# One tile for response and inputs: three sums of 384 columns in the spectral stage

## The chip, the cores and the metric

The kernel runs on one core of a Trainium2 chip. The core has five engines that work side by side, each through its own queue and in order: TensorE (matmuls, PE in the profile; its weight loads are PEld), VectorE (DVE), ScalarE (ACT), GpSimd (POOL) and SyncE (SP), which here only issues transfers. Matmuls read operands from SBUF and write sums to PSUM; ScalarE and VectorE read the sums from there. The metric is device time in microseconds (us); three runs of the kernel before took 1110.23, 1110.36 and 1110.42 us, median 1110.36.

## What is computed

With L = 2048 positions, D = 576 channels, N = 128 states and F = 4608 hidden units:

```python
x = A_u
xn = _layernorm(x, axis=-1)
return x + _A_ref(xn, ...) + _B_ref(xn, B_w1, B_w2)

# _B_ref: out = silu(xn @ w1) @ w2
# _A_ref: a long convolution for each channel
K = jnp.einsum("dn,dnl,dn->dl", Cc, exp(dt * A * l), dB).real
Kf = rfft(K padded to 2 * L)
Uf = rfft(xn padded to 2 * L)
y = irfft(Uf * Kf)[:L] + xn * Dskip
```

Two parts are added: a feed-forward block, which is most of the arithmetic, and a convolution of each channel with its own response K, done through a Fourier transform in stages that are matmuls.

## The kernel before

All large matmuls have float32 operands split in two parts of fewer bits, a high part `h` and a low part `l` (`h` is a rounding copy on ScalarE, `l` the difference on VectorE). A product is then three matmuls: high with high, high with low, low with high.

**The feed-forward block** (`ffn`) goes over two halves of the positions, nine chunks of four 128-wide slices of F, and two blocks of 512 positions. `up` makes a sum `ph` of 14 matmuls, 512 columns wide (lines 331 to 333), ScalarE takes its SiLU (`gf`, line 339) and its high part (`gh`, line 340), VectorE the low part (`gl`, line 342). `down` makes sums `po` of twelve matmuls, 288 columns wide (line 357), and VectorE adds them to `acc` (line 361).

**The convolution** (`side`) is a generator that is woven into the steps of `ffn`: `kgen` makes the response K and its first transform stage into a tensor `d1k` in HBM, `spread` does the first stage of the inputs into `d1u`, `spectral` does the middle of the transform and writes `d2`, `tail` does the last stage and adds the result to the outputs. `marks` and `tail_at` (lines 865 and 866) say at which shares of `ffn`'s steps each part is called. A planner that estimates each instruction's time then sets the order of each engine's queue, so a matmul of `spectral` stands between matmuls of `ffn` wherever the planner put it; `behind` ties an instruction after another one, and `high_priority` moves it up.

**The spectral stage** (`spectral`, line 730) has 32 steps `k`. For each, SyncE loads 128 rows of `d1u` and 128 rows of `d1k` (`load_part`, line 816: tiles `ur` and `kr`, 576 columns each, two buffers). `split_of` (line 809) makes `uh`, `ul`, `kh` and `kl`. `front` (line 735) multiplies both with the step's 128x128 matrix (`mk`, loaded for two steps at once into `mm`). It goes over the halves of the 576 channels, 288 columns (`HD`) each: a sum `pk` of the response, which ScalarE copies out in four pieces of 64 partitions into `ka` and `kb` (lines 750 to 753, a real and an imaginary part in two arrangements), then a sum `pu` of the inputs, which VectorE multiplies with `ka` and `kb` into `y` and `y2` (lines 756 to 758). The sums of `mm3` (line 821) have three matmuls, all recorded at line 826. Then VectorE adds `y` and `y2`, `split_of` splits the result, and one more matrix gives two sums `pb`, which ScalarE copies to `yo` (line 778) and GpSimd's queue writes to `d2`. `front(k + 1)` is called ahead of the `pb` of step `k`.

All sums of this stage take a buffer of the pool `pss`, which has three, a 2 KB bank for each partition: `pk`, `pu`, `pk`, `pu` and two `pb` for each step. `ps1` (two buffers) holds `ph`, `ps2` (three) holds `po`.

The first operands are loaded and split ahead of the others (line 762 and 766), and `ops` holds them for step 0.

Of the kernel before, what the change touches and what calls it, by code (L numbers as in the profile page):

```python
# [11 lines left out]
F32 = mybir.dt.float32  # L12
F32R = mybir.dt.float32r
# [6 lines left out]
P = 128  # L20
L = 2048
D = 576
# [2 lines left out]
NJ = 16  # L25
NKT = 4
HD = D // 2
NFT = FF // P
MAGIC = 12582912.0
TWO_PI = float(np.nextafter(np.float32(2 * math.pi), np.float32(0)))  # L30
# [13 lines left out]
def kernel(  # L44
# [21 lines left out]
    nc = tc.nc  # L66
    FT = 4
    NCH = NFT // FT

# [4 lines left out]
    def quarters(v, engines):  # L74

        for q in range(4):
            yield slice(32 * q, 32 * q + 32), v[q // 2, q % 2], engines[q % len(engines)]

    dram = ctx.enter_context(tc.tile_pool(name="dram", bufs=1, space=DRAM))
    d1u = dram.tile([32 * P, D], F32, name="d1u")  # L80
    d1k = dram.tile([32 * P, D], F32, name="d1k")
# [28 lines left out]
    pss = ctx.enter_context(tc.tile_pool(name="pss", bufs=3, space=PSUM))  # L110
# [31 lines left out]
    def behind(ins):  # L142
        return tc.issue_after(ins) if ins is not None else nullcontext()

    def spread(up):
# [3 lines left out]
        for j in range(NJ):  # L149
            src = up.tile([P, D], F32, tag="xr", name="xr")  # L150
            nc.sync.dma_start(src, dxn[:, j])
            for m in range(2):
# [5 lines left out]
                for h in range(2):  # L158
                    hs = slice(h * HD, (h + 1) * HD)
                    pu = pss.tile([P, 512], F32, tag="pss", name="pu")  # L160
                    nc.tensor.matmul(pu[:, :HD], s1[:, 0, :], sp[:, hs], start=True, stop=False)  # L161
                    nc.tensor.matmul(pu[:, :HD], s1[:, 1, :], sp[:, hs], start=False, stop=True)  # L162
                    nc.scalar.copy(u1[:, hs], pu[:, :HD])
                nc.gpsimd.dma_start(
# [15 lines left out]
    def store(t, j, engines):  # L180

        for hs in (slice(0, HD), slice(HD, D)) if j == NJ - 1 else (slice(0, D),):
            for ps, v, eng in quarters(ov, engines):
                eng.dma_start(v[:, j:j + 2] if len(t.shape) > 2 else v[:, j, hs], t[ps] if len(t.shape) > 2 else t[ps, hs])

    def norm(p0, js, xs):
# [4 lines left out]
        for i in range(n):  # L191
            for h in range(2):
                nc.vector.bn_stats(out=st[:, i, h, :], in_=xs[i][:, h * HD:(h + 1) * HD])
            nc.vector.bn_aggr(out=mv[:, i, :], in_=st[:, i, :, :])
# [253 lines left out]
    kl = yp = pa = tail_at = None  # L448
# [281 lines left out]
    def spectral():  # L730
        def operands(k):
            rows = slice(k * P, (k + 1) * P)
            return load_part(d1u[rows, :], "u"), load_part(d1k[rows, :], "k")

        def front(k):
            if k % 2 == 0:
                mm = kl.tile([P, 2, 4, P], F32R, tag="mm", name="mm")
                nc.gpsimd.dma_start(mm, cm23[:, k:k + 2])
                mats.append(mm)
            mk = mats[-1][:, k % 2]  # L740
            us, ks = ops.pop(k) if k in ops else (split_of(t, n) for t, n in zip(operands(k), "uk"))
            ka = kl.tile([P, D], F32, tag="ka", name="ka")
            kb = kl.tile([P, D], F32, tag="kb", name="kb", bufs=1)
            y = kl.tile([P, D], F32, tag="y", name="y", bufs=1)
            y2 = kl.tile([P, D], F32, tag="y2", name="y2", bufs=1)
            for h in range(2):
                hs = slice(h * HD, (h + 1) * HD)
                pk = pss.tile([P, 512], F32, tag="pss", name="pk")
                mm3(pk[:, :HD], [(mk[:, 0], mk[:, 1], ks)], hs)
                nc.scalar.copy(ka[:64, hs], pk[:64, :HD])  # L750
                nc.scalar.copy(ka[64:, hs], pk[:64, :HD])
                nc.scalar.mul(kb[:64, hs], pk[64:, :HD], -1.0)
                nc.scalar.copy(kb[64:, hs], pk[64:, :HD])
                pu = pss.tile([P, 512], F32, tag="pss", name="pu2")
                mm3(pu[:, :HD], [(mk[:, 0], mk[:, 1], us)], hs)
                nc.vector.tensor_mul(y[:, hs], pu[:, :HD], ka[:, hs])
                nc.vector.tensor_mul(y2[:64, hs], pu[64:, :HD], kb[:64, hs])
                nc.vector.tensor_mul(y2[64:, hs], pu[:64, :HD], kb[64:, hs])
            nc.vector.tensor_add(y, y, y2)
            return mk, split_of(y, "y")  # L760

        mats = []
        first = operands(0)
        yield 1.1
        with behind(pins["gh"]):
            ops = {0: [split_of(t, n) for t, n in zip(first, "uk")]}
        yield 1.12
        nxt = front(0)
        for k in range(32):
            mk, ys = nxt  # L770
            if k < 31:
                nxt = front(k + 1)
            yo = kl.tile([P, D], F32, tag="yo", name="yo")
            for h in range(2):
                hs = slice(h * HD, (h + 1) * HD)
                pb = pss.tile([P, 512], F32, tag="pss", name="pb")
                mm3(pb[:, :HD], [(mk[:, 2], mk[:, 3], ys)], hs)
                nc.scalar.copy(yo[:, hs], pb[:, :HD])
            nc.gpsimd.dma_start(d2.rearrange("(p k) d -> k p d", k=32)[k], yo)
            yield 1 + (k + 1) / 32  # L780
# [26 lines left out]
    yss = {}  # L807

    def split_of(t, tag):
        h = kl.tile([P, D], F32R, tag=tag + "h", name=tag + "h")  # L810
        l = kl.tile([P, D], F32R, tag=tag + "l", name=tag + "l")
        nc.scalar.copy(h, t)
        nc.vector.tensor_sub(l, t, h)
        return h, l

    def load_part(rows, tag):
        t = kl.tile([P, D], F32, tag=tag + "r", name=tag + "r")
        nc.sync.dma_start(t, rows)
        return t

    def mm3(dst, terms, hs):

        n = 0
        for sh, sl, (mh, ml) in terms:
            for st, mv in ((sh, mh), (sh, ml), (sl, mh)):
                nc.tensor.matmul(dst, st, mv[:, hs], start=n == 0, stop=n == 3 * len(terms) - 1)  # L826
                n += 1
# [35 lines left out]
    def side():  # L863
# [66 lines left out]
        with tc.tile_pool(name="kl", bufs=2) as kl:  # L930
            for at in spectral():
                yield marks[1] + (at - 1) * (marks[2] - marks[1])
# [90 lines left out]
```

## Time and profile before

| what | value |
| --- | --- |
| runs, median (lowest to highest) | 1110.36 us (1110.23 to 1110.42) |
| span of the profiled execution, first to last instruction | 1108.2 us |
| granted TensorE clock over the span | 1.000 |
| matmuls of the whole kernel | 9167 |
| matmuls of lines 357 / 331 to 333 | 3456 / 2072 |
| matmuls of line 826, `pk` / `pu` / `pb` | 192 / 192 / 192 |

The profile page gives the span of one profiled execution; its own time outside the span is not listed, and the median of the runs lies 2.16 us above the span. In the profile's rows, `L826 PE MATMUL pk<-kh,mm 128*128 128x288 f32` reads: line 826, TensorE, a matmul that writes `pk` from `kh` and the matrix `mm`, 128 rows by 128 columns of weights, 288 moving columns. In a timeline the first number is the start from the beginning of the span and the second the duration, both in us; rows are merged (x4) where the same instruction follows itself, and what stands in brackets is the engine's idle time before the row and what ended it. In a list of groups the numbers after the bar are the busy time in us, the mean of one in ns, and the idle time before in us. In a list of waits they are the total in us, how often, and the longest. The list of transfers ends each row with the median time in us from issue to landing.

### The profile page before, as it was taken

The page shows a single profiled execution, that of the slowest core. Times are in us where ns is not written, and L with a number is a line of the kernel's source. Part 1 is how long each engine was busy: PE and PEld are TensorE (multiplying, and loading weights), DVE is VectorE, ACT ScalarE, POOL GpSimd, SP SyncE. Part 2 cuts the span into 40 slices and gives each one's busy share as a digit, 9 for nine tenths or more (in the row PEclk, how much of TensorE's full clock was granted, in tenths as well). Part 3 has the DMA queues.
Part 4 walks back from the last instruction along what each step waited for, and adds up shares of the span by engine and source line. Part 5 has one row for each costly group of instructions (what it writes and reads, how often), then busy time and mean ns, then how long its engine had stood idle before and what let it go on. Part 6 is the DMA issues. An engine that isn't in the chain of part 4 may idle for free.

```text
span 1108.2 us, 22917 instructions
## 1 busy us (share of the span) xinstructions
PE 1102.2 (99%) x9167; PEld 997.5 (90%) x9167; DVE 916.6 (83%) x1543; ACT 706.9 (64%) x1222; POOL 72.1 (7%) x129
## 2 busy tenths in 40 slices
PE   9999999999999999999999999999999999999998
PEld 7989998899998899899999989999999999999887
DVE  7799899999999999999999737787778778784433
ACT  4564466676677676677867536877777878774210
POOL 1100000000000000011000000000000000000111
PEclk9999999999999999999999999999999999999999
DMA  9745512525252525264744173554544455434983
GB/s 270 190 123 160 152 50 61 120 73 131 77 121 83 116 72 118 77 174 154 206 122 103 45 179 109 162 167 123 156 145 152 138 149 170 129 107 127 241 224 87
DMA packets 175755, 148.56 MB, mean 134 GB/s; under 512 B 111088, under 2 KB 142592, under 8 KB 175520
## 3 DMA queue, kind: packets, MB, share of 16 engines
q1 hardware_dynamic: 165328, 112.63, 38.7%
q0 software_dynamic: 9568, 33.62, 9.6%
q8 instruction: 72, 1.18, 0.5%
q10 hardware_dynamic: 752, 0.85, 0.3%
q14 instruction: 35, 0.29, 0.1%
HBM read 102.53 MB, written 44.61 MB: 133 GB/s over the span
## 4 chain that ended last, share of the span: by engine, by line
PE 98%; DMA 1%; DVE 1%; SPq 0%; issue 0%; DVEq 0%
PE po L357 42%; PE ph L331 35%; PE kp L696 3%; PE ph L332 3%; PE ph L333 3%; PE pu L826 2%; PE pb L826 2%; PE pk L826 2%; PE z L711 2%; PE pu L161 1%; PE py L847 1%; DMA acc<-in_A_u_dram 1%; PE pu L162 1%; PE pt L124 0%; DVE w1l L295 0%; PE ptk L490 0%
## 5 line engine op out<-in xcount | busy, mean ns | idle before, releaser
L357 PE MATMUL po<-w2l,gh 128*128 128x288 f32 x1152 | 338.5, 295 | 0.0
L357 PE MATMUL po<-w2h,gl 128*128 128x288 f32 x1152 | 336.4, 295 | 0.0
L357 PE MATMUL po<-w2h,gh 128*128 128x288 f32 x1152 | 336.1, 295 | 0.0
L357 PEld LDWEIGHTS po<-w2h,gh 128*128 128x128 f32 x1152 | 215.2, 188 | 7.7 <-issue 2.8
L357 PEld LDWEIGHTS po<-w2l,gh 128*128 128x128 f32 x1152 | 215.9, 188 | 5.1 <-issue 0.5
L357 PEld LDWEIGHTS po<-w2h,gl 128*128 128x128 f32 x1152 | 215.4, 188 | 0.9
L339 ACT ACTIVATE gf<-ph 128x512 f32<-128x512 f32 (+1 forms) x148 | 86.4, 584 | 143.8 <-PE ph L333 134.8
L331 PE MATMUL ph<-xh,w1l 128*128 128x512 f32 (+1 forms) x592 | 161.3, 385 | 0.0
L331 PE MATMUL ph<-xh,w1h 128*128 128x512 f32 (+1 forms) x592 | 161.3, 387 | 0.0
L331 PE MATMUL ph<-xl,w1h 128*128 128x512 f32 (+1 forms) x592 | 161.1, 385 | 0.0
L361 DVE TENSOR_TENSOR acc<-po,acc 128x288 f32<-128x288 f32 x288 | 126.2, 451 | 37.0 <-PE po L357 35.6
L342 DVE TENSOR_TENSOR gl<-gf,gh 128x512 fp32r<-128x512 f32 (+1 forms) x148 | 99.0, 672 | 64.6 <-ACT gh L340 63.8
L331 PEld LDWEIGHTS ph<-xh,w1l 128*128 128x128 f32 x592 | 108.0, 188 | 20.0
L331 PEld LDWEIGHTS ph<-xl,w1h 128*128 128x128 f32 x592 | 107.9, 188 | 19.8
L331 PEld LDWEIGHTS ph<-xh,w1h 128*128 128x128 f32 x592 | 104.5, 188 | 16.7 <-ACT x L133 0.5
L340 ACT CAST gh<-gf 128x512 fp32r<-128x512 f32 (+1 forms) x148 | 89.5, 608 | 9.5 <-PE po L357 6.6
L653 ACT ACTIVATE c<-th,magic 128x1040 f32<-128x1040 f32 x36 | 42.1, 1168 | 37.9 <-DVE C L676 28.0
L655 ACT ACTIVATE c<-th 128x1040 f32<-128x1040 f32 x36 | 38.7, 1075 | 33.6 <-DVE th L654 33.6
L314 ACT CAST w2h<-w2r 128x576 fp32r<-128x576 f32 x72 | 47.0, 671 | 17.7 <-PE po L357 14.9
L295 DVE TENSOR_TENSOR w1l<-w1r,w1h 128x640 fp32r<-128x640 f32 x72 | 56.9, 817 | 0.2
L332 PE MATMUL ph<-x,w1h 128*128 128x512 f32 (+1 forms) x148 | 57.0, 386 | 0.0
L333 PE MATMUL ph<-x,w1l 128*128 128x512 f32 (+1 forms) x148 | 56.9, 385 | 0.0
(185 smaller groups left out, 1828.8 us busy)
## 6 DMA issues: line engine op xcount, KB each, us to landing
w2r<-in_B_w_dram SPq DMA_DIRECT2D x72, 288.0 KB, 3.8
w1r<-in_B_w_dram SPq DMA_DIRECT2D x35, 512.0 KB, 3.8
d1u<-u POOLq DMA_DIRECT2D x32, 288.0 KB, 2.5
d1k<-stage SPq DMA_DIRECT2D x18, 512.0 KB, 6.8
ur<-d1u SPq DMA_DIRECT2D x32, 288.0 KB, 3.7
kr<-d1k SPq DMA_DIRECT2D x32, 288.0 KB, 2.9
d<-yo POOLq DMA_DIRECT2D x32, 288.0 KB, 4.0
ys<-d SPq DMA_DIRECT2D x32, 288.0 KB, 11.8
```

The costliest lines, as they stand in the source:

```text
L295: pins["w1l"] = nc.vector.tensor_sub(l1, src, h1).ins
L314: pins["w2h"] = nc.scalar.copy(h2, r2).ins
L331: nc.tensor.matmul(ph, w[:, kt, :], v[:, kt, a:e], start=n + kt == 0, stop=False)
L332: nc.tensor.matmul(ph, h1[:, 4, :], x4[:, a:e], start=False, stop=False)
L333: pins["pe"] = nc.tensor.matmul(ph, l1[:, 4, :], x4[:, a:e], start=False, stop=True).ins
L339: nc.scalar.activation(gf, ph, AF.Silu)
L340: pins["gh"] = nc.scalar.copy(gh, gf).ins
L342: pins["gl"] = nc.vector.tensor_sub(gl, gf, gh).ins
L357: pins["pe"] = nc.tensor.matmul(po[:, :HD], G[blk, t][g][:, js], W2[half, c, t][w][:, hs], start=n == 0, stop=n == 3 * FT - 1).ins
L361: nc.vector.tensor_add(acc[j][:, hs], po[:, :HD], acc[j][:, hs])
L653: nc.scalar.activation(c65, th, AF.Identity, bias=magic)
L826: nc.tensor.matmul(dst, st, mv[:, hs], start=n == 0, stop=n == 3 * len(terms) - 1)
```

## The change

Response and inputs of a step are loaded into the two halves of one tile `ukr` of 2 x 576 columns, the response first; `split_of` takes the tile's shape and splits all 1152 columns with one cast and one subtraction into `ukh` and `ukl`. `front` makes three sums of 384 columns (`DA`) over these 1152: the first is response alone, the second holds the last 192 columns of the response and the first 192 of the inputs, the third is inputs alone. ScalarE copies out the response's part of a sum in the same four pieces, now 384 and 192 columns wide, and VectorE multiplies the inputs' part, 192 and 384 columns wide. What follows from `y` on stays.

```diff
+DA = 2 * D // 3
...
         def operands(k):
             rows = slice(k * P, (k + 1) * P)
-            return load_part(d1u[rows, :], "u"), load_part(d1k[rows, :], "k")
+            t = kl.tile([P, 2, D], F32, tag="ukr", name="ukr")
+            nc.sync.dma_start(t[:, 0], d1k[rows, :])
+            nc.sync.dma_start(t[:, 1], d1u[rows, :])
+            return t.rearrange("p i d -> p (i d)")
...
-            us, ks = ops.pop(k) if k in ops else (split_of(t, n) for t, n in zip(operands(k), "uk"))
+            both = ops.pop(k) if k in ops else split_of(operands(k), "uk")
...
-            for h in range(2):
-                hs = slice(h * HD, (h + 1) * HD)
-                pk = pss.tile([P, 512], F32, tag="pss", name="pk")
-                mm3(pk[:, :HD], [(mk[:, 0], mk[:, 1], ks)], hs)
-                nc.scalar.copy(ka[:64, hs], pk[:64, :HD])
-                nc.scalar.copy(ka[64:, hs], pk[:64, :HD])
-                nc.scalar.mul(kb[:64, hs], pk[64:, :HD], -1.0)
-                nc.scalar.copy(kb[64:, hs], pk[64:, :HD])
-                pu = pss.tile([P, 512], F32, tag="pss", name="pu2")
-                mm3(pu[:, :HD], [(mk[:, 0], mk[:, 1], us)], hs)
-                nc.vector.tensor_mul(y[:, hs], pu[:, :HD], ka[:, hs])
-                nc.vector.tensor_mul(y2[:64, hs], pu[64:, :HD], kb[:64, hs])
-                nc.vector.tensor_mul(y2[64:, hs], pu[:64, :HD], kb[64:, hs])
+            for c in range(3):
+                cs = slice(c * DA, (c + 1) * DA)
+                pk = pss.tile([P, 512], F32, tag="pss", name="pku")
+                mm3(pk[:, :DA], [(mk[:, 0], mk[:, 1], both)], cs)
+                if c < 2:
+                    hs = slice(c * DA, min((c + 1) * DA, D))
+                    n = hs.stop - hs.start
+                    nc.scalar.copy(ka[:64, hs], pk[:64, :n])
+                    nc.scalar.copy(ka[64:, hs], pk[:64, :n])
+                    nc.scalar.mul(kb[:64, hs], pk[64:, :n], -1.0)
+                    nc.scalar.copy(kb[64:, hs], pk[64:, :n])
+                if c:
+                    hs = slice(max(c * DA - D, 0), (c + 1) * DA - D)
+                    pu = pk[:, DA - (hs.stop - hs.start):DA]
+                    nc.vector.tensor_mul(y[:, hs], pu, ka[:, hs])
+                    nc.vector.tensor_mul(y2[:64, hs], pu[64:], kb[:64, hs])
+                    nc.vector.tensor_mul(y2[64:, hs], pu[:64], kb[64:, hs])
...
-            ops = {0: [split_of(t, n) for t, n in zip(first, "uk")]}
+            ops = {0: split_of(first, "uk")}
...
     def split_of(t, tag):
-        h = kl.tile([P, D], F32R, tag=tag + "h", name=tag + "h")
-        l = kl.tile([P, D], F32R, tag=tag + "l", name=tag + "l")
+        h = kl.tile(list(t.shape), F32R, tag=tag + "h", name=tag + "h")
+        l = kl.tile(list(t.shape), F32R, tag=tag + "l", name=tag + "l")
         nc.scalar.copy(h, t)
         nc.vector.tensor_sub(l, t, h)
         return h, l
-
-    def load_part(rows, tag):
-        t = kl.tile([P, D], F32, tag=tag + "r", name=tag + "r")
-        nc.sync.dma_start(t, rows)
-        return t
```

## The prediction, made before the changed kernel was run

> **What bounds the kernel now.** I read the page first: the busy line, then the chain that ended last.
>
> ```profile
> span 1108.2 us, 22917 instructions
> PE 1102.2 (99%) x9167; PEld 997.5 (90%) x9167; DVE 916.6 (83%) x1543; ACT 706.9 (64%) x1222; POOL 72.1 (7%) x129
> ...
> PE 98%; DMA 1%; DVE 1%; SPq 0%; issue 0%; DVEq 0%
> ```
>
> TensorE is busy for 99% of the span and is 98% of the chain. A busy PE isn't yet a PE at its peak, so the next views are the waits of PE over the whole span and the busy time of the stage that the change touches, whose ends are the first `pk` and the last `pb` matmul.
>
> ```profile
> L826 PE MATMUL pk<-kh,mm x128: 288/294/304, 674.7 to 997.3; 128*128 128x288 f32 x128
> ...
> L826 PE MATMUL pb<-yh,mm x128: 288/294/301, 689.4 to 1009.6; 128*128 128x288 f32 x128
> ...
> PE pz L879 <- DVE zero L874: 1.3, 1, 1.3
> PE pt L124 <- DVE xn L202: 0.4, 2, 0.2
> 674.00:1011.00 337.00, 337.00 (x2132) 313.48 (x2131) 262.87 (x480) 255.00 (x534) 24.54 (x46) 1.00 0.47 139
> ```
>
> The second pair of rows is the whole list of PE's waits: three, 1.7 us together, none of them for anything of this stage. The last row is the stage (columns: PE, PEld, DVE, ACT, POOL, then the granted clock, which is 1.00): 2132 matmuls, no idle time at all, with VectorE at 263 of 337 us and ScalarE at 255. So here a microsecond counts only if it is TensorE's, and work saved on VectorE or ScalarE buys nothing by itself.
>
> Next I need what a matmul costs TensorE, which is the distance from one start to the next, not the duration printed (a 288-column matmul is printed with 0.29 us, but they overlap). From the timeline of TensorE:
>
> ```profile
> 14.07 0.64 PE L331 MATMUL ph<-xh,w1h 128*128 128x256 f32 x4
> ...
> 15.98 0.74 PE L331 MATMUL ph<-xh,w1l 128*128 128x256 f32 x4
> ...
> 649.73 0.29 PE L357 MATMUL po<-w2h,gh 128*128 128x288 f32 x1
> ...
> 653.97 1.08 PE L331 MATMUL ph<-xh,w1h 128*128 128x512 f32 x4
> ...
> 657.15 0.29 PE L357 MATMUL po<-w2h,gh 128*128 128x288 f32 x1
> ...
> 765.76 0.30 PE L826 MATMUL pk<-kh,mm 128*128 128x288 f32 x1
> ...
> 766.94 1.08 PE L331 MATMUL ph<-xh,w1h 128*128 128x512 f32 x4
> ```
>
> Between the second pair of rows lie 32 matmuls of 288 columns: 4.24 / 32 = 0.1325 us each. Then 14 of 512 columns: 3.18 / 14 = 0.2271. The first pair encloses 16 of 256 columns: 1.91 / 16 = 0.1194. The last pair encloses nine of the stage's own, 288 wide: 1.18 / 9 = 0.1311. The line through 288 and 512 has a slope of (227.1 - 132.5) / 224 = 0.422 ns a column and a fixed part of 132.5 - 288 x 0.422 = 10.9 ns; it gives 0.1190 at 256, where 0.1194 was seen. So time is columns plus about 11 ns for each matmul.
>
> **The change, part by part.** *The sums.* Before, one of the 32 steps makes four sums of three matmuls, 12 x 288 = 3456 columns. After, three sums of three, 9 x 384 = 3456 columns: the same columns, three fixed parts fewer. At 384 columns the line gives 132.5 + 96 x 0.422 = 173.0 ns. A step goes from 12 x 132.5 = 1590 to 9 x 173.0 = 1557 ns: 33 ns less, and 32 x 33 ns = 1.05 us over the stage. No 384-column matmul stands in the trace, so both ends: drawn from the stage's own 131.1, the slope is 0.429, a 384 is 172.2 and the gain 32 x (1573 - 1550) = 0.7 us; at the price of a 512 (the nearest wider row) nine cost 2044 ns and the stage loses 32 x 454 = 14.5 us; nine at the price of a 288, as the other end, would gain 32 x 397 = 12.7 us. Three widths on one line put the value at the line, and I take 1.05.
>
> The Trainium skill (TensorE: Matmul & The Clock Gate, "Wait — 56ns, not 53.3ns?") gives a fixed cost of about 2.5 ns a matmul over N / 2.4 GHz; by that, an estimate, the gain would be 32 x 3 x 2.5 ns = 0.24 us. The trace differs here, with 10.9 ns where every matmul has its own weight load, and the measurement decides.
>
> *The splits.* Two casts and two subtractions of 576 columns become one of each of 1152 columns.
>
> ```profile
> L812 ACT CAST kh<-kr 128x576 fp32r<-128x576 f32 x32 | 21.5, 673 | 0.7
> ...
> L813 DVE TENSOR_TENSOR kl<-kr,kh 128x576 fp32r<-128x576 f32 x32 | 24.2, 758 | 31.6 <-ACT kh L812 31.6
> L653 ACT ACTIVATE c<-th,magic 128x1040 f32<-128x1040 f32 x36 | 42.1, 1168 | 37.9 <-DVE C L676 28.0 <-DVE th L639 9.7
> L637 DVE TENSOR_TENSOR th<-vt,fT 128x1040 f32<-128x1040 f32 x36 | 44.4, 1235 | 0.1
> L293 ACT CAST w1h<-w1r 128x640 fp32r<-128x640 f32 x72 | 48.8, 725 | 3.3 <-DMA w1r<-in_B_w_dram 3.2
> L703 ACT COPY kt<-kp 128x512 f32<-128x512 f32 x18 | 10.3, 574 | 15.2 <-PE kp L696 15.2
> L750 ACT COPY ka<-pk 64x288 f32<-64x288 f32 x64 | 25.1, 392 | 16.0 <-PE pk L826 15.1
> ```
>
> VectorE: from 576 to 1040 columns the slope is (1235 - 758) / 464 = 1.03 ns, so 1152 take about 1.35 us in place of 2 x 0.758: 0.17 us less a step, 5 us over the stage. ScalarE: the cast's slope from 576 to 640 is 0.81 ns, so 673 + 576 x 0.81 = 1.14 us (1.26 by the 1040 row) in place of 1.35: 3 to 7 us less. Both are hidden behind TensorE's 337 us and cost or gain nothing; what they change is that the single pieces are longer, by 0.59 us on VectorE and 0.47 on ScalarE. Also `kl` may not start before the whole cast ends. Whether this delays a sum is read from how early the operands are ready:
>
> ```profile
> 782.82 0.76 DVE L813 TENSOR_TENSOR kl<-kr,kh 128x576 fp32r<-128x576 f32 x1 [0.19 <-ACT kh L812]
> ...
> 785.28 0.76 DVE L813 TENSOR_TENSOR ul<-ur,uh 128x576 fp32r<-128x576 f32 x1
> ...
> 797.99 0.30 PE L826 MATMUL pk<-kh,mm 128*128 128x288 f32 x1
> ...
> 798.39 0.30 PE L826 MATMUL pu<-uh,mm 128*128 128x288 f32 x1
> ```
>
> Counted in order, these are the thirteenth split pair and the thirteenth sums: `kl` is done 14.4 us and `ul` 12.4 us ahead of its matmul. The new single split must now be whole before the first sum, which takes about 2 us of these 12. Zero, then; with the cover gone, every step would pay its cast and subtraction, 2.5 us.
>
> *The loads.* The same two transfers of 288 KB a step, response first, into the halves of one tile. Both wait for one buffer, freed by the one long subtraction, where each had its own.
>
> ```profile
> SPq L818 <- DVE kl L813: 145.9, 30, 7.4
> ...
> SPq L818 <- DVE ul L813: 52.3, 25, 3.5
> ur<-d1u SPq DMA_DIRECT2D x32, 288.0 KB, 3.7
> kr<-d1k SPq DMA_DIRECT2D x32, 288.0 KB, 2.9
> ```
>
> SyncE's queue stands already 55 times in those waits, and the weight loads `w1r` and `w2r` wait behind it; now it stands about 31 times, each at most a long subtraction (1.35 us) later. A landing takes 2.9 to 3.7 us, far inside the 12 us. Zero; bare, 3.7 us a step. At the stage's start the first pair can't begin before the response is complete in HBM, and both halves were needed then too.
>
> *The evictions.* ScalarE still makes eight copies a step and VectorE six products, now 384 and 192 wide in place of 288 and 288; with a linear cost that is the same time. PSUM buffers taken: five a step in place of six. Before, the fourth sum had to wait for a buffer (three exist), which now falls away; TensorE filled that time with other matmuls, so it gains nothing. One thing is new: the middle tile holds 192 columns of the response, read by ScalarE, and 192 of the inputs, read by VectorE. If the two readers are kept in turn, VectorE's products wait for up to four copies: 392 - 96 x 0.81 = 314 ns each by the two copy rows, 1.26 us. The lower bound is nothing. The Trainium skill (PSUM — Partial Sum Buffer, "PSUM bank collisions raise a hardware error") has two engines reading one bank and quadrant at once as an error, which speaks for the turn; no tile of the stage has two readers in this trace, so it doesn't show it.
>
> Sum: -1.05 us on TensorE, the rest zero. Against the profiled execution: 1108.2 - 1.05 = 1107.15 us of span. The median run, 1110.36 us, lies 2.16 above that span, and I carry this over unchanged: **1109.3 us**, -0.09%.
>
> **The rivals.** *Slower, by a stall behind the longer pieces.* VectorE and ScalarE take their work in order. A piece that waits or runs longer delays what is queued behind it: the `gl` subtraction that the down matmuls need, and the `acc` additions that free their PSUM buffers. The tightest places of the stage:
>
> ```profile
> 741.42 0.69 DVE L342 TENSOR_TENSOR gl<-gf,gh 128x512 fp32r<-128x512 f32 x1 [0.52 <-ACT gh L340]
> 743.55 0.29 PE L357 MATMUL po<-w2h,gl 128*128 128x288 f32 x1
> 807.26 0.69 DVE L342 TENSOR_TENSOR gl<-gf,gh 128x512 fp32r<-128x512 f32 x1
> 808.64 0.29 PE L357 MATMUL po<-w2h,gl 128*128 128x288 f32 x1
> 940.00 0.69 DVE L342 TENSOR_TENSOR gl<-gf,gh 128x512 fp32r<-128x512 f32 x1 [0.52 <-ACT gh L340]
> 941.63 0.29 PE L357 MATMUL po<-w2h,gh 128*128 128x288 f32 x1
> ...
> 942.03 0.29 PE L357 MATMUL po<-w2h,gl 128*128 128x288 f32 x1
> ```
>
> Each pair is a block's last `gl` and, counted in order, the matmul that reads it: margins of 1.44, 0.69 and 1.34 us. The worst added hold is the longer cast, the longer subtraction and the wait for the middle tile: 0.47 + 0.59 + 1.26 = 2.3 us. Caught by all of it, the three places stall 0.9 + 1.6 + 1.0 = 3.5 us, and the time is 1109.3 + 3.5 = **1112.8**. It decides from a hold of 0.7 us on. For it: VectorE stood 31.6 us waiting for `kh` casts already (the row of `kl` above). Against it: the order of the queues is planned anew with the new pieces, and in 337 us the old order never came to a stall.
>
> *The width is off the line.* A 384-column matmul at the price of 512 gives 1110.36 + 14.5 = **1124.9**. Three widths on one line speak against it.
>
> *Nothing comes of it.* The 33 ns a step are real, but TensorE's new order gives them back, in small late starts that no wait shows, or in more changes between whole-array and tiled matmuls further on. Such a change costs about 0.1 us:
>
> ```profile
> 1033.16 0.40 PE L357 MATMUL po<-w2h,gh 128*128 128x288 f32 x1
> 1033.40 0.29 PE L357 MATMUL po<-w2l,gh 128*128 128x288 f32 x1
> ```
>
> Here 0.24 us pass between the starts where 0.13 is usual, right after tiled matmuls. Ten more of them eat the gain: **1110.4**. The same mechanism in the other direction, some fifteen fewer, would give 1109.3 - 1.5 = **1107.8**.
>
> **How the numbers follow.** The forecast has a chance of 0.60, nothing 0.11, the stall 0.20, the width 0.03, fewer changes of mode 0.06. About 0.2% (2.2 us) can be told from no change, so forecast and nothing are "same"; only the last case, 1107.8, reaches past it on the fast side. Faster 0.06, same 0.71, slower 0.23. The range reaches down to 1107.8, the case of fewer mode changes, and up to 1113.4, a little past the stall; the price of a 512 stays outside.
>
> **What would show it.** In the changed profile: 9071 matmuls in place of 9167; 288 with 384 columns, starting 0.173 us apart; PE without a wait between 674 and 1010; the last matmul of the stage about 1 us earlier; one 1152-column cast near 1.14 and subtraction near 1.35 us a step, some 12 us ahead of their sums. A wait of PE for `acc`, `gl` or `y` in the stage would make the stall right; starts 0.22 us apart, the width. A stage shorter by over 2 us would make me wrong on what TensorE pays for.

## The result, and the profile after

The changed kernel takes 1112.81 us (median of 15 runs, 1112.0 to 1113.65); the kernel before, run beside it, 1110.36 (15 runs, 1109.91 to 1111.86). The ratio is 1.0021, with a 95% interval of 1.0014 to 1.0029: 2.45 us slower. The time lies inside the forecast range, but on the other side of the kernel before than its middle.

The page of the kernel after, its span, its busy line and the shares of its chain of waits:

```profile
span 1111.0 us, 22619 instructions
...
PE 1103.5 (99%) x9071; PEld 997.5 (90%) x9071; DVE 910.2 (82%) x1511; ACT 698.3 (63%) x1190; POOL 72.7 (7%) x129
...
PE 88%; DVE 6%; ACT 3%; issue 1%; DMA 1%; SPq 0%; DVEq 0%
```

96 matmuls fewer, as computed, and still a longer span. The busy share doesn't show why; the chain does. TensorE fell from 98% of it to 88%, and VectorE and ScalarE now stand in it with 9%. So somewhere TensorE is released by them. The list of TensorE's waits over the whole span (total in us, how often, longest), and below it the stage's row of busy times (PE, PEld, DVE, ACT, POOL, granted clock):

```profile
PE pz L882 <- DVE zero L877: 1.3, 1, 1.3
PE pt L125 <- DVE xn L203: 0.7, 2, 0.5
PE pb L829 <- ACT gh L341: 0.5, 1, 0.5
PE po L358 <- ACT w2h L315: 0.4, 1, 0.4
PE pb L829 <- ACT yo L786: 0.2, 1, 0.2
674.00:1014.00 340.00, 339.18 (x2041) 314.26 (x2040) 257.99 (x451) 246.76 (x505) 24.79 (x46) 1.00 0.49 151
```

Two waits of `pb` are new. The stage, without a hole before, has 0.82 us of idle TensorE, at full clock. The holes are bigger when read as distances between starts, because a matmul is printed longer than the time it occupies TensorE. By that measure five `pb` sums start late, 1.53 us together beyond the usual 0.13 each, at 883.3, 924.8, 933.1, 953.4 and 961.2 us.

How much of the loss lies in the stage? The order of TensorE's queue is the same in both kernels ahead of 669 us and behind 1027 us. So two matmuls found in both give a fair stretch. First the kernel before, then after, each in TensorE's timeline:

```profile
668.13 0.39 PE L333 MATMUL ph<-x,w1l 128*128 128x512 f32 x1
...
1051.34 0.30 PE L357 MATMUL po<-w2h,gl 128*128 128x288 f32 x1
```

```profile
668.89 0.39 PE L334 MATMUL ph<-x,w1l 128*128 128x512 f32 x1
...
1054.17 0.30 PE L358 MATMUL po<-w2h,gl 128*128 128x288 f32 x1
```

383.21 us before, 385.28 after: 2.07 us are lost in the stretch that holds the stage. The other 0.76 us of the longer span were lost ahead of it. 0.66 of them are one stop at 441 us, where the cast `w2h` waits for its transfer (the `po` row of the waits above). The queue of TensorE is still the same there as before. Over the kernels below, the size of this stop varied between 0 and 0.9 us from profile to profile: 0.5 us in a kernel with four sums (the one with the later mark), none in two kernels with three sums (split in halves, `pb` from the other pool), and 0.9 in one that is as fast as the kernel before. So nothing here ties it to the change.

**What stalls.** TensorE's timeline of the kernel after around the first of the five, cut to the sums of the stage and the matmul ahead of the hole:

```profile
879.83 0.29 PE L358 MATMUL po<-w2l,gh 128*128 128x288 f32 x1
...
880.09 0.34 PE L829 MATMUL pku<-ukh,mm 128*128 128x384 f32 x1
880.27 0.34 PE L829 MATMUL pku<-ukl,mm 128*128 128x384 f32 x1
880.45 0.34 PE L829 MATMUL pku<-ukh,mm 128*128 128x384 f32 x1
...
881.15 0.30 PE L829 MATMUL pb<-yh,mm 128*128 128x288 f32 x1
...
882.48 0.29 PE L358 MATMUL po<-w2h,gl 128*128 128x288 f32 x1
883.32 0.37 PE L829 MATMUL pb<-yh,mm 128*128 128x288 f32 x1 [0.55 <-ACT gh L341]
```

The first `pb` sum of the step (881.15) starts on time; the second (883.32) comes 0.84 us after the matmul ahead of it in place of 0.13. The profile names `gh` as the releaser, but this matmul doesn't read `gh`. What it needs is a PSUM buffer. `pss` has three, handed out in the order in which the program asks: the three sums of step k + 1, then the two `pb` of step k. So the second `pb` takes the buffer of the middle tile, and the middle tile has two readers. Here they are, ScalarE first, then VectorE:

```profile
880.25 0.47 ACT L760 COPY kb<-pku 64x384 f32<-64x384 f32 x1
880.75 0.31 ACT L757 COPY ka<-pku 64x192 f32<-64x192 f32 x1
881.07 0.31 ACT L758 COPY ka<-pku 64x192 f32<-64x192 f32 x1
881.40 0.33 ACT L759 ACTIVATE kb<-pku 64x192 f32<-64x192 f32 x1
881.73 0.31 ACT L760 COPY kb<-pku 64x192 f32<-64x192 f32 x1
```

```profile
882.08 0.36 DVE L764 TENSOR_TENSOR y<-pku,ka 128x192 f32<-128x192 f32 x1 [2.77 <-ACT kb L760]
882.45 0.36 DVE L765 TENSOR_TENSOR y<-pku,kb 64x192 f32<-64x192 f32 x1
882.82 0.35 DVE L766 TENSOR_TENSOR y<-pku,kb 64x192 f32<-64x192 f32 x1
```

ScalarE finishes the copies of the first tile, makes the four of the middle tile one after the other, and ends at 882.04. VectorE, which had stood 2.77 us, starts 0.04 later, and its third product ends at 883.17. The second `pb` starts 0.15 us behind that. Before, the second `pb` took the buffer of the second `pk`, which ScalarE alone read. Now three products stand behind the copies: 357 + 359 + 351 ns by the groups below, about 1.1 us more until the buffer is free. In two of the five places (924.8 and 953.4) VectorE has two products of the third tile in its queue ahead of these three, and at 933.1 an `acc` addition between them, which holds the buffer still longer. The long cast and the long subtraction are not in the way: at none of the five does `ukh` stand in ScalarE's queue ahead of the middle tile's copies, or `ukl` in VectorE's ahead of its products, between the end of the middle sum and its third product.

The groups of the stage by form (busy us, mean ns of one, idle before, and its cause) have the predicted durations and the standing time:

```profile
L821 DVE TENSOR_TENSOR ukl<-ukr,ukh 128x1152 fp32r<-128x1152 f32 x32 | 43.4, 1356 | 1.0 <-ACT ukh L820 0.4
L820 ACT CAST ukh<-ukr 128x1152 fp32r<-128x1152 f32 x32 | 37.0, 1157 | 0.5
...
L765 DVE TENSOR_TENSOR y<-pku,kb 64x192 f32<-64x192 f32 x32 | 11.5, 359 | 0.4
L764 DVE TENSOR_TENSOR y<-pku,ka 128x192 f32<-128x192 f32 x32 | 11.4, 357 | 34.6 <-ACT kb L760 34.2
L766 DVE TENSOR_TENSOR y<-pku,kb 64x192 f32<-64x192 f32 x32 | 11.2, 351 | 0.4
L760 ACT COPY kb<-pku 64x192 f32<-64x192 f32 x32 | 10.0, 314 | 0.5
```

VectorE stood 34.2 us for the last copy of the middle tile. In none of the 32 steps does its first product start earlier than 0.03 us behind ScalarE's fourth copy, though `ka` and `kb` of the first columns are ready long before. The readers are kept in turn. It isn't `ka` as a whole over which they are kept apart: in the kernel before, ScalarE starts to copy into the second half of `ka` before VectorE's products with the first half end, in 29 of 32 steps. What the two share here is the tile in PSUM. The Trainium skill (PSUM — Partial Sum Buffer, "PSUM bank collisions raise a hardware error") has the compiler's scheduler put a dependency between any two instructions on different engines that touch the same bank and quadrant of PSUM, reads against reads too; the 34.2 us agree.

**The stage also moved.** The list of the tile `pb`, its first and last start:

```profile
L829 PE MATMUL pb<-yh,mm x128: 288/295/378, 689.7 to 986.8; 128*128 128x288 f32 x128
```

31 steps lie between them: (986.8 - 689.7) / 31 = 9.58 us a step. Before it was (1009.6 - 689.4) / 31 = 10.33 by the row in the prediction. As I read it, the planner starts a step as soon as its estimates allow; with three sums that take three buffers, in place of four, the chain of a step is shorter, and the stage ends 23 us earlier. What that does to the buffers is the margin of the second `pb`: its start minus the end of the last reader of its buffer, in us, worked out from the timelines for steps 15 to 30.

```
before 1.82 2.80 3.14 1.77 1.16 3.22 2.26 2.66 2.71 2.72 1.82 2.29 2.65 3.21 2.07 2.71
after  2.69 2.32 0.43 0.31 0.71 0.15 0.37 1.41 1.33 0.15 0.15 0.59 0.15 0.15 1.71 0.90
```

Before, the smallest of all 31 is 1.16. After, the margin drops from step 17 on, and five times it is 0.15, the least that either profile of this kernel shows: there TensorE stands. In a second profile of the same kernel the same five steps stand, and the margins agree within 0.02 us.

### The profile page after: what moved, and what is told of

Same layout as the page of the kernel before. It is cut to its first block, busy times and chain, and to the rows that moved or that the text cites. A ratio compares the mean times of both kernels' runs of the same rounds, so it can differ in the third digit from the quotient of the medians.

```text
span 1111.0 us, 22619 instructions
## 1 busy us (share of the span) xinstructions
PE 1103.5 (99%) x9071; PEld 997.5 (90%) x9071; DVE 910.2 (82%) x1511; ACT 698.3 (63%) x1190; POOL 72.7 (7%) x129
## 3 DMA queue, kind: packets, MB, share of 16 engines
q8 instruction: 71, 1.16, 0.4%
## 4 chain that ended last, share of the span: by engine, by line
PE 88%; DVE 6%; ACT 3%; issue 1%; DMA 1%; SPq 0%; DVEq 0%
PE po L358 38%; PE ph L332 32%; PE pku L829 4%; PE kp L697 3%; PE ph L333 3%; PE ph L334 3%; PE pb L829 2%; PE z L712 2%; PE pu L162 1%; PE py L850 1%; DMA acc<-in_A_u_dram 1%; PE pu L163 1%; DVE ukl L821 1%; DVE w1l L296 1%; DVE y L767 0%
## 5 line engine op out<-in xcount | busy, mean ns | idle before, releaser
L340 ACT ACTIVATE gf<-ph 128x512 f32<-128x512 f32 (+1 forms) x148 | 86.3, 584 | 142.9 <-PE ph L334 132.5
L764 DVE TENSOR_TENSOR y<-pku,ka 128x192 f32<-128x192 f32 (+1 forms) x64 | 29.1, 456 | 45.5 <-ACT kb L760 34.2
L829 PE MATMUL pku<-ukh,mm 128*128 128x384 f32 x192 | 61.5, 337 | 0.0
L317 DVE TENSOR_TENSOR w2l<-w2r,w2h 128x576 fp32r<-128x576 f32 x72 | 53.5, 750 | 6.8 <-ACT w2h L315 6.0
```

What stands on the lines that cost most here:

```text
L317: pins["w2l"] = nc.vector.tensor_sub(l2, r2, h2).ins
L340: nc.scalar.activation(gf, ph, AF.Silu)
```

## The experiments

Three theories stood against one another: the buffer of the middle tile with its two readers in turn; the long cast and subtraction, behind which other work queues; and the closer steps, with the earlier end of the stage. "The stretch" is the distance between the two matmuls shown above, 383.21 us before and 385.28 after. Diffs are against the kernel after, where nothing else is said.

### Four sums from the joint tile

```diff
-            for c in range(3):
...
+            for h in range(2):
+                pk = pss.tile([P, 512], F32, tag="pss", name="pk")
+                mm3(pk[:, :HD], [(mk[:, 0], mk[:, 1], both)], hs)
...
+                pu = pss.tile([P, 512], F32, tag="pss", name="pu2")
+                mm3(pu[:, :HD], [(mk[:, 0], mk[:, 1], both)], slice(D + h * HD, D + (h + 1) * HD))
```

> The changed kernel with its one tile, one cast and one subtraction of 1152 columns, but the four sums of 288 columns of the kernel before, each with one reader. Theory A (the middle tile, read first by ScalarE and then by VectorE, comes free too late, and the second pb sum, whose turn it is for that buffer, waits on TensorE): no stall of TensorE in the stage, 9167 matmuls, 1110.4 us, within 0.5. Theory B (the long cast and subtraction hold up the queues of ScalarE and VectorE): the long pieces are still there, so it stays near 1112.5 us.

1114.69 us, ratio 1.0041 (1.0029 to 1.0054). The stage's row, and behind it the wait that it has instead:

```profile
674.00:1018.00 344.00, 344.00 (x2183) 320.19 (x2182) 262.29 (x455) 250.50 (x504) 24.26 (x45) 1.00 0.43 137
...
PE py L846 <- DMA ys<-d: 4.2, 1, 4.2
```

With the joint tile and the long split, but without a tile of two readers, the stage has no hole. So the long split alone doesn't stall it. The joint tile and the long split together do lengthen a step: the last `pb` starts at 1017.0 us, 7.4 later than before, and the transform's last stage, which reads back what the spectral stage wrote, waits 4.2 us for its input `ys`. At that stop the granted clock falls to 0.50, from 1038.7 to 1045.4 us. That is a new loss of another kind. (The profile is of the slowest of the five runs, 1117.12 us.)

### Split in halves, three sums

```diff
+        for i in range(t.shape[1] // D):
+            c = slice(i * D, (i + 1) * D)
+            nc.scalar.copy(h[:, c], t[:, c])
+            nc.vector.tensor_sub(l[:, c], t[:, c], h[:, c])
```

> The changed kernel with its one tile and three sums, but the split done in two halves of 576 columns (two casts, two subtractions, 0.67 and 0.76 us each). Theory A: the middle tile is as before, so most of the stall stays: 1112 to 1112.8 us, second pb sums still start within 0.2 us of the release by VectorE's third product. Theory B: the stall is gone and the fewer matmuls show: 1109.9 us.

1114.23 us, ratio 1.0034 (1.0021 to 1.0046). The `pb` stalls stay, at five places, but they are 0.82 us in place of 1.53. The rest was lost behind the stage, in one wait of TensorE and, as its cause, one of ScalarE:

```profile
PE po L358 <- ACT gh L341: 1.9, 1, 1.9
...
1011.17 0.67 ACT L315 CAST w2h<-w2r 128x576 fp32r<-128x576 f32 x1 [7.87 <-DMA w2r<-in_B_w_dram]
```

ScalarE works in order, so `gf` and `gh`, which the down sums need, stand behind a `w2h` cast whose weights land late. The stage ends at 985.6 here, and the loads of `ys` for the last stage are issued while the last weights are still to come. SyncE's timeline of the kernel after has the same mixture:

```profile
998.77 0.58 SPq L838 DMA_DIRECT2D ys<-d  x1
999.46 0.54 SPq L306 DMA_DIRECT2D w2r<-in_B_w_dram  x1
1000.04 0.58 SPq L838 DMA_DIRECT2D ys<-d  x1
...
1005.84 9.02 SPq L838 DMA_DIRECT2D ys<-d  x7
1016.38 0.33 SPq L306 DMA_DIRECT2D w2r<-in_B_w_dram  x1
```

There ScalarE stood 4.7 us for `w2r` without TensorE noticing. In the second profile of that kernel, below, it stood 5.7 us and TensorE lost 0.3. So an early end is no gain by itself; it brings a risk at the end.

### The sums `pb` from the other pool

```diff
-                pb = pss.tile([P, 512], F32, tag="pss", name="pb")
+                pb = ps2.tile([P, 512], F32, tag="ps2", name="pb")
```

> The changed kernel with the two pb sums of a step in buffers of the pool of the down sums (ps2) in place of the pool of the spectral sums (pss); the middle tile and the long split stay. Theory A: pb no longer stands behind the middle tile's release; 1109.9 us (9 x 175 against 12 x 132.5 ns a step gives 0.5 us less than before), no waits of PE for it in the stage. Theory B: the long pieces still hold up what TensorE needs: 1112 us or more.

1158.04 us, ratio 1.0435 (1.0421 to 1.045). The longest waits of TensorE are another kind:

```profile
PE pb L829 <- ACT yh L820: 9.6, 4, 5.9
PE po L358 <- ACT w2h L315: 5.3, 1, 5.3
```

With `pb` in the pool of the down sums the whole order changes; why these waits arise was not followed up. This says nothing about the middle tile: a miss.

### ScalarE copies the inputs' part of the middle tile too

```diff
+                    if c == 1:
+                        um = kl.tile([P, DA // 2], F32, tag="um", name="um")
+                        nc.scalar.copy(um, pu)
+                        pu = um
```

> The changed kernel with one more copy a step: ScalarE copies the inputs' 192 columns of the middle tile to SBUF (0.31 us), and VectorE's products of that part read the copy, so the middle tile has one reader and comes free without VectorE. Theory A: the tile is free at least 0.8 us earlier after its last copy (three products of 0.36 less one copy of 0.31), the stall is mostly gone: 1110.0 to 1110.6 us. Theory B: no change, 1112.5 us.

1121.03 us, ratio 1.0096 (1.0082 to 1.011). With one reader, the holes ahead of `pb` shrink to 0.61 us at three places, 0.40 of it at one (by the distance between starts, less what is usual behind the matmul ahead), though the steps come closer still, 9.08 us apart (the stage's last `pb` at 972.3). The price comes at the end again, and larger:

```profile
1006.36 0.29 PE L358 MATMUL po<-w2l,gh 128*128 128x288 f32 x1
1009.54 2.07 PE L332 MATMUL ph<-xh,w1h 128*128 128x512 f32 x4 [2.89 <-ACT gf L340]
1011.42 1.91 PE L332 MATMUL ph<-xl,w1h 128*128 128x512 f32 x4
```

ScalarE had stood 8.9 us for `w2r`, and 3.2 us pass on TensorE between two starts. What comes then runs at half the pace: the rows of two stretches have a granted clock (third number from the end) of 0.50 behind the stop and 1.00 again later.

```profile
1009.50:1015.40 5.90, 5.86 (x14) 4.60 (x15) 1.67 (x3) 1.74 (x3) 0.00 (x0) 0.50 1.06 304
1016.00:1020.00 4.00, 3.10 (x22) 2.63 (x21) 1.51 (x3) 1.79 (x3) 0.00 (x0) 1.00 0.15 49
```

### `pb` ahead of the next step's sums

```diff
-            if k < 31:
-                nxt = front(k + 1)
             yo = kl.tile([P, D], F32, tag="yo", name="yo")
...
+            if k < 31:
+                nxt = front(k + 1)
             yield 1 + (k + 1) / 32
```

> The changed kernel with the two pb sums of step k written ahead of the three sums of step k + 1, so pb takes buffers that have long been free, and no sum stands behind the middle tile of the next step. Theory A (the second pb sum stands behind the middle tile): no wait of TensorE for pb within the stage; but the steps overlap less, the stage ends about 33 us later (294 up and down matmuls later in the queue), close to the tail, and whatever is lost moves there: 1111 to 1118 us, all of the stalls after the stage. Theory B (long pieces): stalls within the stage as in the changed kernel, about 2 us, whatever the order.

1240.48 us, ratio 1.1176 (1.1161 to 1.1191). Until 1000 us no `pb` stood for its buffer, as the order of the pool says. But without the next step's sums between `y` and `pb` a step takes so long that the stage outlasts the feed-forward block; TensorE then waits 70.4 us for `yh` in 13 places, and from 1010 us to the end of the stage its granted clock is 0.50. Only the first part counts for the question.

### The end of the stage marked later, with and without the change

Kernel after:

```diff
-        marks = (0.13, 0.597, 0.823)
+        marks = (0.13, 0.597, 0.90)
```

> The changed kernel with the end of the stage's share of the steps moved from 0.823 to 0.90: the queue of TensorE then has the last pb 75 matmuls later than in the changed kernel (still 78 ahead of the kernel before). Theory C (three sums shorten a step's chain, the planner packs the 32 steps closer, 43 in place of 48 up and down matmuls apart, and the margins of the second pb sum shrink to nothing): the wider spacing lets part of the stall go, 1110.3 to 1111.8 us. Against C: the spacing doesn't matter, 1112.8 us.

1113.84 us, ratio 1.0033 (1.0021 to 1.0046). My idea that the later mark would space the steps was wrong. The holes ahead of `pb` grew to 2.38 us at seven places. The planner set the steps as close as before, and the first margin of 0.15 comes at step 6 already. At one of the seven places, 854.3 us, the profile itself names VectorE's third product (`y`, line 766) as what ended the wait. Only the last three, which the mark itself held back, have margins of 3.35, 2.00 and 2.01 us. Those three were the hint: where a step is held back, its margin returns.

Kernel before:

```diff
-        marks = (0.13, 0.597, 0.823)
+        marks = (0.13, 0.597, 0.88)
```

> The kernel before with the end of the stage's share at 0.88: control for the run above, four sums and two splits. The last pb is 54 matmuls later. No stall within the stage by any theory; the stage's end comes 7 us nearer to the tail, as in the run with four sums and the long split, where the tail stood 4.3 us for the transfers of d2. If that is the price of a late end, 1113 to 1115 us; if it belonged to the long split, 1110.4 us.

1114.62 us, ratio 1.0037 (1.0024 to 1.0049). No hole in the stage, and 3.4 us of waiting for `ys` behind it, with the granted clock at 0.50 for 3.4 us after the stop. A late end costs at the last stage whatever the sums look like, which is what the four sums from the joint tile had shown.

### The kernel after once more

> The changed kernel once more, for a second profile. Its 0.68 us stop of TensorE at 441 us lies in a part where the order of TensorE's queue is that of the kernel before. If it is chance, it is not there again or is elsewhere; if it belongs to the kernel, it is at the same matmul. The waits of the second pb sum are at the same steps, from the eighteenth on, 1112.8 us.

1112.38 us, ratio 1.0020 (1.0011 to 1.0029). The holes ahead of `pb` are 1.52 us at the same five steps; the stop at 441 us is 0.89 here. The stretch is 385.58 us, 0.31 longer than in the first profile, by the late `w2r` at the end. The loss is a property of the plan, not of one execution.

### The steps held apart

Each step is now released at its own share, and the end is marked later:

```diff
-            yield 1 + (k + 1) / 32
+            yield 1.12 + 0.88 * (k + 1) / 32
...
-        marks = (0.13, 0.597, 0.823)
+        marks = (0.13, 0.597, 0.905)
```

> The changed kernel with the 32 steps handed to the planner evenly (1.12 + 0.88 (k + 1) / 32 of the stage's share, whose end goes from 0.823 to 0.905), so that a step is written down only when the up and down work has come that far: the last pb stands 123 matmuls later in TensorE's queue than in the changed kernel, 30 ahead of the kernel before, and the queue of the transfers at the tail has the order of the kernel before. Theory C, mended (the planner starts each step as soon as the step before lets it, so the second pb sum stands right behind the middle tile; in the last run only the last steps were held back, and their margins alone grew, to 2 us and more): the margins of the second pb sum are 1 us and more at nearly all steps, no wait of TensorE in the stage, 1109.6 to 1110.3 us. Against: the margins stay at 0.15 us and the time at 1112.5 us or more.

1110.57 us beside 1110.51 for the kernel before, ratio 1.0002 (0.9993 to 1.001). Three sums, the long split and the two readers in turn are all still there, and the loss is gone. The steps are (1005.7 - 697.3) / 31 = 9.95 us apart. From step 14 on no margin of the second `pb` is under 0.87, and one hole of 0.31 us is left, at step 6. The stretch is 383.52 us, 0.31 over before.

> As the run with evenly handed steps, and the split in two halves of 576 columns. If the long pieces cost anything once the steps are held back, this is faster than the run with evenly handed steps by up to 1 us; if the middle tile's release under close steps was all, the two are equal within 0.5 us, 1109.6 to 1110.3 us.

The same with the split in halves: 1110.38 us, ratio 0.9999 (0.9991 to 1.0008), no hole in the stage, and no margin under 1.2 us.

The control is the kernel before with the same two lines:

> The kernel before with its steps handed to the planner evenly and the share's end at 0.905: control for the two evenly handed runs. Its steps are longer, the last pb stands 54 matmuls later than before and 84 later than in the evenly handed changed kernel, so the first py sums stand for their transfers: 1113 to 1115 us, all of the loss after the stage.

1114.52 us, ratio 1.0045 (1.0032 to 1.0058), with 2.4 us of waiting for `ys`. So the spacing isn't a gain that any kernel would have. With four sums the last `pb` then starts at 1017.2 us, as late as in the two kernels above that waited for `ys`; with three it starts at 1005.7.

### The readers of the middle tile swapped

VectorE's products of the middle tile are put ahead of ScalarE's copies of it:

```diff
-                if c < 2:
+                if c == 0:
...
                     nc.vector.tensor_mul(y2[64:, hs], pu[:64], kb[64:, hs])
+                if c == 1:
+                    hs = slice(c * DA, min((c + 1) * DA, D))
+                    n = hs.stop - hs.start
+                    nc.scalar.copy(ka[:64, hs], pk[:64, :n])
...
```

> The changed kernel with VectorE's three products of the middle tile written ahead of ScalarE's four copies of it. If the two readers of the tile are kept in turn whichever comes first, ScalarE's copies now wait for VectorE's third product, and VectorE no longer for ScalarE's last copy of 192 columns; the tile comes free about as late, and the second pb sum waits for that: 1112 to 1114 us. If the readers aren't kept in turn (VectorE only waited for the ka and kb that it needs), neither waits for the other, and the waits stay as in the changed kernel.

1114.16 us, ratio 1.0032 (1.0021 to 1.0042). The stage's row, and two of its waits:

```profile
674.00:1000.00 326.00, 326.00 (x1974) 303.51 (x1973) 257.43 (x445) 244.04 (x498) 24.79 (x46) 1.00 0.48 150
...
ACT ka L770 <- DVE y L766: 8.5, 14, 1.0
```

The turn shows from the other side. ScalarE now stands for VectorE's third product, and in none of the 32 steps does the first copy start before it ends. The wait of 34.2 us for the last copy is gone, since the products need only the first tile's copies: the program's order of the readers decides which of them waits. The holes are gone too, with steps 9.52 us apart, (984.6 - 689.6) / 31, a little closer than after; every margin of the second `pb` is 1.8 us or more. What this profile loses is lost where the splits in halves lost theirs: the stage ends early, `w2h` waits 7.19 us for `w2r`, and TensorE stands behind it. (The profile is of a run of 1112.55 us; why the median run is 1.6 us longer isn't shown.)

```profile
1011.33 0.40 PE L358 MATMUL po<-w2h,gh 128*128 128x288 f32 x1 [1.20 <-ACT gh L341]
```

### Both cures

The swapped readers and the steps held apart, in one kernel (the two diffs above).

> The changed kernel with both cures at once: VectorE's products of the middle tile ahead of ScalarE's copies of it (no wait of TensorE in the stage in the run with that alone, but 1.4 us at its end for weights queued behind the transfers of d2), and the steps handed over evenly up to 0.905 (the order of the transfers at the tail is then that of the kernel before). If the order of the two readers and the early end of the stage are the whole loss, nothing is left of it and the fewer matmuls show: no wait of TensorE between 674 and 1031 us, 1109.9 us (0.5 less than before, from 9 x 175 against 12 x 132.5 ns a step). If a third cause is left, 1111 us or more.

1110.43 us beside 1110.57, ratio 0.9998 (0.9989 to 1.0007). The stage has no hole:

```profile
674.00:1011.00 337.00, 337.00 (x2035) 313.30 (x2034) 260.66 (x452) 250.43 (x506) 24.87 (x46) 1.00 0.45 142
```

The stretch is 383.00 us, 0.21 under the kernel before in these single profiles. That is the sign and about the size of what three sums save on TensorE, but two profiles of the kernel after differ by 0.31, and in the runs' time it can't be told from nothing. No kernel of the study beats the kernel before beyond its interval.

## Why the prediction was right or wrong

**What TensorE pays for: right, and too large.** Of the sum, the term "33 ns a step" was mis-sized. The mean distance from the start of one of the stage's `pk`, `pu` or `pku` matmuls to the next start is 132.3 ns over 384 matmuls before and 175.2 over 288 after, in place of the 132.5 and 173.0 of the line. 384 x 132.3 = 50.80 us against 288 x 175.2 = 50.45: 0.35 us saved, not 1.05. The line through 288 and 512 missed the point between them by 2.2 ns, and a difference of small numbers doesn't forgive that. By the fixed cost of about 2.5 ns that the Trainium skill gives (TensorE: Matmul & The Clock Gate, "Wait — 56ns, not 53.3ns?"), the prediction had 0.24 as an estimate. That gain was nearer, although the cost of a single matmul isn't that of the page: over its N / 2.4 GHz the 132.3 ns are 12.3 more at 288 columns and the 175.2 are 15.2 more at 384. The width rival (a 384 at the price of a 512) is refuted.

**The splits: right in the main.** 1.157 us for the cast and 1.356 for the subtraction against 1.14 and 1.35, done 7 to 13 us ahead of their first sum in all steps but the first. The joint tile and the long split alone leave the stage without a hole. What the text called hidden isn't quite free, though: with four sums the two made the stage end 7.4 us later, past what the last stage can bear.

**The evictions: here the prediction failed.** The step that failed is "the rest zero" in its sum, for the PSUM buffers. It foresaw that VectorE might wait for up to four copies, 1.26 us, and took that for a wait of VectorE, which reached TensorE only through `gl` or `acc` in its stall rival. Of the buffers it wrote "PSUM buffers taken: five a step in place of six", and that this "gains nothing". It counted the buffers and didn't ask who takes the middle tile's buffer next. That is the second `pb`, and for it the hold is the four copies and the three products in a row, with what stands ahead of them in the two queues: at the five places 5.3 to 8.1 us from the end of the middle sum to the end of the third product. In place of nothing this term cost 1.53 us of holes on TensorE, and about 1.9 us with the late starts behind them. The swap of the readers and the single reader show it as the cause, each in its own way, at steps that are closer still: the holes of 1.53 us go to 0 and 0.61.

**The stall rival: right time, other mechanism.** It gave 1112.8 us and the kernel took 1112.81, but by chance. It summed 0.47 + 0.59 + 1.26 of hold against margins of `gl`; none of those places stood. The split's 1.06 us of it stood at none of the five places, and alone, with four sums, it stalls nothing. With three sums, halving it went with smaller holes (0.82 in place of 1.53, and none in place of 0.31 with the steps held apart); since each of these kernels was planned anew, a small part of the split's isn't excluded. Its argument against itself, that in 337 us the old order never came to a stall, was weak: the old order isn't kept.

**What the prediction didn't see: the stage moves.** It expected "the last matmul of the stage about 1 us earlier". It is 22.8 us earlier, since the planner sets a shorter step closer to the one before. Its sign "a stage shorter by over 2 us would make me wrong on what TensorE pays for" therefore pointed to the wrong term: TensorE pays 0.35 us less, and the rest of the 22.8 is `ffn` work that now stands behind the stage. Three products take about 1.1 us off margins that were 1.16 at the least, so at the old pace hardly one would have reached the floor; that much is argued. Shown is that holding the steps apart removes all holes but one, with the sums, the split and the readers unchanged. So both are needed, the readers in turn and the closer steps: to shorten the turn or to space the steps, each alone, removes nearly all of the holes.

**The account.** 1.53 us of holes, each followed by a start some 0.08 us late (0.4 together), another 0.3 at a `ph` sum at 941.7 us and the start behind it, less 0.35 saved: about 1.9 of the 2.07 us. That `ph` starts 0.05 us after ScalarE's `gf`, which stood behind the middle tile's copies. The other 0.2 is spread over many small differences, none over 0.06 us.

**Open.** Why the margins fall only from step 17 on: what the planner estimates for each release isn't in the trace. And the late `w2r` at the end of the stage: that an early end mixes `ys` loads with the last weights is seen in SyncE's order, and the wait comes in all three of the kernels whose time went there (split in halves, single reader, swap), but the order of these loads was not changed by itself. The kernel after ends as early and lost nothing there in one profile and 0.3 us in the other.

## What to carry to other kernels

Follow each PSUM buffer to its next user: when a tile gets a second reader on another engine, the time until it is free is the sum of both, in turn, with whatever their queues hold in between, and whoever takes the buffer next pays. Where a planner fills a queue, a shorter step isn't the same plan with shorter pieces; it moves work closer and earlier, so look at the margins (start minus release) at the new pace and at the transfers that the earlier end brings forward, and hold the steps apart if need be. And where TensorE has no holes, a gain of a third of a microsecond is smaller than the first hole that the change can open.

## What the hardware showed that I had not expected

- The least time from the end of the last reader of a PSUM buffer to the start of the matmul that takes it was 0.146 to 0.148 us, in all ten places of the two profiles of the kernel after where TensorE stood for it. The last reader there is on VectorE. With a ScalarE copy as the last reader (the kernel with the single reader) it was 0.05 us at three places.
- The releaser that the profile names for a late `pb` (`gh`, `yo`) was in the kernel after not the instruction that it waited for. The end of the third product, 0.15 us ahead each time, was.
- One stop of 3.2 us between two starts was followed by 5.9 us at a granted clock of 0.50, with matmuls of 512 columns 0.43 us apart in place of 0.227. The Trainium skill (TensorE: Matmul & The Clock Gate, "What's actually happening") has half rate after an idle window of about 3.4 us; the row agrees with the half rate, but these runs give no such length. Behind the stage, stops of 3.2, 3.8 and 4.6 us between starts were followed by a granted clock of 0.50 and one of 2.8 us was not, while in the kernel with `pb` from the other pool half clock came at 702.2 us, after a stop of 1.6 us. The stop of 3.2 us cost some 2.7 us more than its length: 14 matmuls took 5.9 us, where 14 x 0.227 is 3.2.
